# Sparse attention and a soft mixture of experts on one core: where token sums are made, which PSUM banks the plain chunk writes, and which rows of v are kept

## The chip, the cores and the metric

The kernel runs on one core of one Trainium2 chip. The metric is the device time of one execution in microseconds; the figure of the kernel before is the median of three runs. An execution taken by the hardware profiler gives the trace. PE is TensorE (PEld its weight loads), DVE VectorE, ACT ScalarE, POOL GpSimd, SP SyncE; an engine's name with a q at its end means what that engine's queue issues.

## The reference

Batch 4, 8 heads, 768 tokens, head dimension 64, key blocks of 32 tokens (24 blocks). Every query block sees its neighbours, the first and the last block and three sampled blocks; the first and the last query block see everything. The attention output, 3072 tokens of 512 numbers, then goes through four experts of 512 x 1024 x 512, each with a relu, and is summed with the normalised domain probabilities.

```python
mask = np.abs(blk_i - blk_j) <= window
mask = mask | (blk_i == 0) | (blk_j == 0) | (blk_i == n_blocks - 1) | (blk_j == n_blocks - 1)
...
attn = np.exp(scores)
attn = attn / (np.sum(attn, axis=-1, keepdims=True) + 1e-09)
return np.matmul(attn, v).astype(np.float32)
...
for e in range(E):
    h = np.maximum(x @ w1[e], 0.0)
    out += p[:, e:e + 1] * (h @ w2[e])
```

## The kernel before, in words

**Stages.** The attention of batch 0 runs alone. Then a stream of expert work for batch b is interleaved with the attention of batch b + 1, by a fixed cost per piece (`T1` for a piece of the first layer, `T2` for one of the second; `drive`). The experts of batch 3 run alone at the end. From line 673 on every engine keeps the program's order, so what is written earlier stands earlier in each engine's queue.

**The attention** works by units: four edge units (first and last query block) and twelve group units (six groups `t` of up to four query blocks, two halves of the heads). A unit has scores `S` (L251, L256), transposes `T`, the product with v `A` (L291) and the transpose of the output `X`, which ends in the token tile `xr` (L312, L372). A query block's keys come in eight slots of 32 keys: three neighbours, first block, last block, three sampled ones. `copy_k` (L113) copies the five latter into `kr`; `load_v` (L124) fills v tiles for two query blocks at a time: the neighbours by one transfer on SP (L130), the first block's rows by another (L133), and the last block's and the sampled blocks' rows by one indirect gather per query block on GpSimd (L136, 128 rows, indices in `vidx`). The tiles come from a pool that rotates six of them in batch 0 (`v1`, L60) and three later (L733). `load_batch` (L78) takes two tiles of the same pool for the whole v of the batch, which the edge units read. `vidx`, the mask `bad` and the index tile `sbt` are set up ahead of all this (L69 to L218).

**The experts.** Each batch has eight chunks (an expert's 1024 hidden numbers in two). Matmul operands are split into a high part and a rest, and a product is three matmuls (L534 to L539). Chunk 0 is the plain chunk: eight products of two halves each, 16 pieces, on four token operands `xo` 1, 2, 7 and 3. Chunks 1 to 7 save multiplications by sums: 7 products for each of two `s`, on seven token operands, of which 4, 5, 6 and a new 7 are differences of token quarters (`conversion`, L390). `conversion` is a generator of 14 steps. Steps 1 to 6 make the operands 2, 1, 7, 3; steps 7 to 12 make 5, 6 and 4: casts on ScalarE (L399), differences on VectorE or GpSimd (L402), subtractions in place on VectorE (L417, L422, L425, L428). Steps 13 and 14 write operand 7 anew. `convert` (L445) takes the next step, up to a limit.

**The order** is made by `experts` (L619). `one` lists the 114 pieces of the first layer, `two` the 192 of the second (`po` banks, L595, collected into `oacc` by VectorE, L608 and L610). The first 12 pieces of `one` come ahead of any second-layer piece; from there the two mix. When `one` is over, every other second-layer piece takes a step of the next batch's conversion (L638), up to 12. In the first layer every piece below 28 takes a step ahead of its matmuls (L642). For batch 0 three steps are taken in the attention (L722) and two behind it (L743, L744).

**Banks.** After the attention of batch 0, PSUM has two banks for scores, one for attention outputs, and in `ps_m2` one each called v and w, and three called po. The plain chunk writes v and w in turn (L551). When a product is done, `finish` (L541) makes `hh` on ScalarE and `hl` on VectorE out of the bank; only then can the bank take another product. Product i of the plain chunk is pieces 2i and 2i + 1. After products 3, 4, 6 and 7 two weight slabs `wo` are made for later (ScalarE cast L493, GpSimd difference L494); seven slabs are ahead.

```python
ORDER = [(s, n) for s in range(2) for n in (2, 1, 5, 6, 3, 7, 4)]
FIRST = [((0, 0, 0), 0), ((0, 1, 0), 0), ((1, 0, 0), 0), ((0, 0, 1), 2), ((0, 1, 1), 2),
         ((1, 1, 0), 0), ((1, 0, 1), 2), ((1, 1, 1), 2)]
XOF = {(0, 0): 1, (1, 0): 2, (0, 1): 7, (1, 1): 3}
```

Of the kernel before, what the change touches and what calls it, by code (L numbers as in the profile page):

```python
# [8 lines left out]
F32 = mybir.dt.float32  # L9
F32R = mybir.dt.float32r  # L10
I32 = mybir.dt.int32
U32 = mybir.dt.uint32
AF = mybir.ActivationFunctionType
ALU = mybir.AluOpType
# [3 lines left out]
P = 128  # L18
# [5 lines left out]
def attention_moe_kernel(ctx: ExitStack, tc, qb, kb, vr, sampled, sampled_t, probs, w1, w2, out):  # L24
# [42 lines left out]
    sbi = p1.tile([NB, NR, 2], I32, name="sbi")  # L67
    nc.scalar.dma_start(sbi, sampled.bitcast(I32).rearrange("n (r t) -> n r t", t=2))
    sbt = p1.tile([NR + 1, NB, 2], I32, name="sbt")  # L69
    nc.scalar.dma_start(sbt[1:], sampled_t.bitcast(I32).rearrange("r (n t) -> r n t", t=2))  # L70
    sbrow = const.tile([1, NB * NR, 2], I32, name="sbrow")
    nc.scalar.dma_start(sbrow, sampled.bitcast(I32).rearrange("n (r t) -> (n r) t", t=2).unsqueeze(0))

    keys = {}
    gathered = {}
    regs = {}

    def load_batch(b):  # L78
        k = gp.tile([P, NB, P], F32, name="k", bufs=1)
        q = gp.tile([P, 2, P], F32, name="qe", bufs=1)  # L80
        for m in range(2):
            ns = slice(m * NB // 2, (m + 1) * NB // 2)
            nc.sync.dma_start(k[:, ns], kb[b, :, ns])
            if m == 0:
                nc.sync.dma_start(q, qb[b, :, 0:NB:NB - 1])
        vs = []
        for m in range(0, KT, 4):
            n = min(4, KT - m)
            v = pool["v"].tile([P, 2, 2, DM], F32, name="v").rearrange("p a b e -> p (a b) e")
            nc.sync.dma_start(v[:, :n], vr[b * S + P * m:b * S + P * (m + n)]  # L90
                              .rearrange("(k p) e -> p k e", p=P))
            vs += [v[:, i] for i in range(n)]
        keys[b] = k, q, vs
# [13 lines left out]
    def sampled_block(j, r):  # L107
        if (j, r) not in regs:
            regs[j, r] = COPIERS[r % len(COPIERS)].value_load(sbrow[:1, j * NR + r, :1],
                                                              min_val=0, max_val=NB - 1)  # L110
        return regs[j, r]

    def copy_k(b, t, cs=range(QG)):  # L113
        for c, j in enumerate(blocks(t)):
            if c in cs:
                k = pool["k"].tile([P, SLOTS - 3, P], F32, name="kr")
                nc.gpsimd.tensor_copy(k[:, :2], keys[b][0][:, 0:NB:NB - 1])
                for r in range(NR):
                    eng = COPIERS[r % len(COPIERS)]
                    copy = eng.copy if eng is nc.scalar else eng.tensor_copy  # L120
                    copy(k[:, 2 + r:3 + r], keys[b][0][:, bass.ds(sampled_block(j, r), 1)])
                gathered[b, t][1][c] = k

    def load_v(b, t, cs=range(QG)):  # L124
        js = blocks(t)
        for c in range(min(cs), min(max(cs) + 1, len(js)), 2):
            n = min(2, len(js) - c)
            v = pool["v"].tile([P, 2, 2, DM], F32, name="v")
            rows = vr[b * S + (js[c] - 1) * BLOCK:b * S + (js[c] + 2) * BLOCK]
            nc.sync.dma_start(v[:3 * BLOCK, :n, 0],  # L130
                              bass.AP(rows.tensor, rows.offset,
                                      [[DM, 3 * BLOCK], [BLOCK * DM, n], [1, DM]]))
            nc.sync.dma_start(v[3 * BLOCK:, :n, 0],  # L133
                              vr[b * S:b * S + BLOCK].unsqueeze(1).broadcast_to([BLOCK, n, DM]))
            for i in range(n):
                nc.gpsimd.indirect_dma_start(  # L136
                    out=v[:, i, 1], out_offset=None, in_=vr, element_offset=b * S * DM,
                    in_offset=bass.IndirectOffsetOnAxis(ap=vidx[:, js[c + i]:js[c + i] + 1], axis=0))
                gathered[b, t][2][c + i] = v[:, i]


# [16 lines left out]
    nc.gpsimd.affine_select(out=lead, in_=lead, pattern=[[-1, P]], compare_op=ALU.is_ge,  # L158
                            fill=0.0, base=BLOCK - 1, channel_multiplier=BLOCK)
    slot = p1.tile([NR + 1, NB], F32, name="slot")  # L160
    nc.gpsimd.memset(sbt[:1], NB - 1)
    nc.vector.tensor_copy(slot, sbt[:, :, 0])
    within = p1.tile([P, 1], F32, name="within")
    nc.gpsimd.iota(within, pattern=[[0, 1]], base=0, channel_multiplier=1,
# [20 lines left out]
    nc.gpsimd.memset(bad, 0.0)  # L185
    nc.vector.tensor_copy(sbf, sbi[:, :, 0])
    nc.vector.tensor_scalar(bad[:, 3:4], nidx, 1.0, None, op0=ALU.is_le)
    nc.vector.tensor_scalar(bad[:, 4:5], nidx, float(NB - 2), None, op0=ALU.is_ge)
    nc.vector.tensor_scalar(d, sbf, nidx, None, op0=ALU.subtract)
    nc.vector.tensor_mul(d, d, d)  # L190
    nc.vector.tensor_scalar(bad[:, 5:], d, 1.0, None, op0=ALU.is_le)
    nc.vector.scalar_tensor_tensor(d, sbf, float(NB - 1), sbf, op0=ALU.subtract, op1=ALU.mult)
    nc.vector.scalar_tensor_tensor(bad[:, 5:], d, 0.0, bad[:, 5:], op0=ALU.is_equal, op1=ALU.max)
    for r in range(1, NR):
        for e in range(r):
            nc.vector.scalar_tensor_tensor(bad[:, 5 + r:6 + r], sbf[:, r:r + 1], sbf[:, e:e + 1],
                                           bad[:, 5 + r:6 + r], op0=ALU.is_equal, op1=ALU.max)

    ind = p1.tile([NB, NG, P], F32, name="ind")
    nc.gpsimd.memset(ind, 1.0)  # L200
# [237 lines left out]
        xr.pop(b)  # L438
        yield

    EARLY, PLAIN = 3, 12
    pieces = {}
    steps = {}

# [78 lines left out]
    def first(b, c, s, n):  # L523
        ps_m, cp, hp = later["m"], later["c"], later["h"]
        if c == 0:
            half, k, g = n
            w, x = wo[b, c, s, (half, k)], xo[XOF[k, g]]
            if g:
                wo.pop((b, c, s, (half, k)))
        else:  # L530
            w, x = wo.pop((b, c, s, n)), xo[n]

        def product(ps, fresh):
            m = 0  # L534
            for t in range(KH):
                for wi, xi in ((0, 0), (1, 0), (0, 1)):
                    nc.tensor.matmul(ps, w[:, wi, t], x[:, xi, t], start=fresh and m == 0,  # L537
                                     stop=m == 3 * KH - 1, skip_group_check=not fresh)
                    m += 1  # L539

        def finish(half, g, src):  # L541
            hh = hp.tile([P, HS], F32R, name=f"hh{g}", bufs=NH[g])
            hl = hp.tile([P, HS], F32R, name=f"hl{g}", bufs=NH[g])
            nc.scalar.activation(hh, src, AF.Relu)  # L544
            nc.vector.scalar_tensor_tensor(hl, src, 0.0, f32(hh), op0=ALU.max, op1=ALU.subtract)  # L545
            hs[c, 2 * s + half, g] = (hh, hl)

        if c == 0:
            i = [item for item, _ in FIRST].index((s, half, g))
            if k == 0:  # L550
                W[0] = ps_m.tile([P, HS], F32, name="vw"[i % 2], bufs=1)  # L551
            product(W[0], k == 0)
            if k == 1:
                finish(half, g, W.pop(0))
                for _ in range(FIRST[i][1]):
                    next(weights, None)
            return
        if n in (5, 2, 3):
            v = ps_m.tile([P, HS], F32, name="v", bufs=1)
            product(v, True)  # L560
        else:
            if n == 1:
                W[s] = ps_m.tile([P, HS], F32, name="w", bufs=1)
            product(W[s], n == 1)
        if n == 2:
            pt[s] = cp.tile([P, HS], F32, name="p1", bufs=1)
            nc.scalar.copy(pt[s], v)
        elif n == 1:
            nc.vector.tensor_add(pt[s], W[s], pt[s])  # L569
            finish(0, 0, pt[s])  # L570
        elif n == 5:
            zt[s] = cp.tile([P, HS], F32, name="z1", bufs=1)
            nc.scalar.copy(zt[s], v)
        elif n == 6:
            ut[s] = cp.tile([P, HS], F32, name="u1", bufs=1)
            nc.vector.tensor_add(ut[s], W[s], zt[s])
        elif n == 3:
            nc.vector.tensor_add(ut[s], v, ut[s])
            finish(0, 1, ut[s])
        elif n == 7:  # L580
            nc.vector.tensor_add(zt[s], W[s], zt[s])
            finish(1, 1, zt[s])
        else:
            finish(1, 0, W[s])
        next(weights, None)
# [33 lines left out]
    def experts():  # L619

        L = len(ORDER)
        for b in range(B):
# [7 lines left out]
            while q < len(two):  # L630

                wait = after_first and p < len(one) and one[p][2] == 4 and q < ready(p - MORE)
                if wait or p >= min(len(one), (q * NCH * L + (OFF + MORE) * len(two)) / len(two)):
                    second(b, *two[q])
                    q += 1
                    after_first = False
                    if p == len(one) and q % 2:
                        convert(b + 1)  # L638
                    yield T2, 2
                else:  # L640
                    if p < 2 * L:
                        convert(b, PLAIN if p <= L else PLAIN + 2)  # L642
                    first(b, *one[p])
                    p += 1
                    after_first = True
                    yield T1, 1
# [177 lines left out]
```

## Time and profile before

| what | value |
|---|---|
| median of the runs | 1311.59 us (three runs, 1309.81 to 1313.77) |
| profiled execution | 1304.3 us, span 1302.6 us |
| mean granted clock of TensorE | 0.992 |
| busy: TensorE, VectorE, ScalarE, GpSimd | 1252.1, 715.6, 622.6, 659.1 us |
| attention of batch 0 alone | to about 95 us |
| starts of the plain chunk | 96.35, 411.15, about 725 and 1040 us |

The page's second part shows the whole run in 40 slices of 32.6 us. TensorE is short of full in the first four slices and just behind batches' ends.

```profile
PE   7678999999998999999999899999999999999998
...
PEclk9989999999999999999999999999999999999999
DMA  8843334353325124443425231443441322222211
```

A row of the timeline gives the start in us, the duration, the engine, the line, the operation with output and inputs, how many were merged, and in brackets the idle time ahead of it with what ended it. A row of waits gives total, times and longest. A row of windows gives the stretch, its length, busy time and instructions of PE, PEld, DVE, ACT and POOL, the granted clock, the mean busy share of the transfer engines, and GB/s.

### The profile page before, as it was taken

How to read it: one execution, taken by the hardware profiler on the slowest of the kernel's cores; microseconds unless marked ns; L12 is line 12 of the kernel's file. 1: busy time of each engine (PE TensorE's matmuls, PEld its weight loads, DVE VectorE, ACT ScalarE, POOL GpSimd, SP SyncE). 2: the span in 40 equal slices, each digit the busy share in tenths (PEclk: the TensorE clock that was granted, in tenths of full speed). 3: DMA queues.
4: the chain of work that ended last, by engine and by line, in shares of the span. 5: the costliest groups of instructions: out<-in, count | busy, mean ns of one | idle time of the engine just before them, and what ended most of it. 6: DMA issues, size and time to landing. Idle time of an engine off the chain costs nothing.

```text
span 1302.6 us, 31439 instructions
## 1 busy us (share of the span) xinstructions
PE 1252.1 (96%) x12286; PEld 1080.3 (83%) x12286; DVE 715.6 (55%) x1690; ACT 622.6 (48%) x1642; POOL 659.1 (51%) x848
## 2 busy tenths in 40 slices
PE   7678999999998999999999899999999999999998
PEld 4557888888887888888888878888888888888887
DVE  5555655655555555655554555556555545555553
ACT  4673445555543445555554344455554434444441
POOL 5543545566445346654545454566553635454551
PEclk9989999999999999999999999999999999999999
DMA  8843334353325124443425231443441322222211
GB/s 257 240 137 113 91 98 124 113 155 103 98 81 191 49 82 118 136 128 99 145 66 174 97 90 34 139 139 123 123 123 37 105 74 65 65 65 66 65 49 57
DMA packets 60048, 140.49 MB, mean 108 GB/s; under 512 B 7163, under 2 KB 8700, under 8 KB 59900
## 3 DMA queue, kind: packets, MB, share of 16 engines
q1 hardware_dynamic: 52816, 115.41, 28.3%
q0 software_dynamic: 7040, 23.07, 6.4%
q8 instruction: 96, 1.57, 0.5%
q14 instruction: 52, 0.43, 0.1%
q10 hardware_dynamic: 44, 0.00, 0.0%
HBM read 132.17 MB, written 6.29 MB: 106 GB/s over the span
## 4 chain that ended last, share of the span: by engine, by line
PE 90%; DVE 6%; issue 2%; ACT 2%; DVEq 0%; DMA 0%; ACTq 0%
PE po L595 40%; PE w L537 20%; PE v L537 15%; PE o L291 4%; PE tp L278 3%; PE s L256 2%; PE s L251 2%; PE sw L325 1%; DVE oacc L610 1%; DVE xo L402 1%; PE ow L356 1%; PE x L310 1%; DVE hl L545 1%; PE tw L346 1%; DVE xr L422 1%
## 5 line engine op out<-in xcount | busy, mean ns | idle before, releaser
L494 POOL TENSOR_TENSOR wo<-r,wo 128x256 fp32r<-128x256 f32 x368 | 288.8, 788 | 412.0 <-ACT wo L493 411.1
L595 PE MATMUL po<-h,hh 128*128 128x512 f32 x768 | 311.4, 405 | 3.7 <-DVE oacc L610 2.1
L537 PE MATMUL w<-xo,wo 128*128 128x384 f32 x1536 | 310.8, 339 | 1.3 <-DVE hl L545 1.3
L595 PE MATMUL po<-h,hl 128*128 128x512 f32 x768 | 303.9, 396 | 0.0
L595 PE MATMUL po<-l,hh 128*128 128x512 f32 x768 | 303.7, 395 | 0.0
L537 PEld LDWEIGHTS w<-xo,wo 128*128 128x128 f32 x1536 | 275.1, 189 | 22.2 <-DVE hl L545 1.7
L537 PE MATMUL v<-xo,wo 128*128 128x384 f32 x1200 | 244.3, 341 | 13.3 <-DVE hl L545 12.2
L537 PEld LDWEIGHTS v<-xo,wo 128*128 128x128 f32 x1200 | 217.3, 190 | 31.5 <-DVE hl L545 13.8
L493 ACT CAST wo<-r 128x256 fp32r<-128x256 f32 x368 | 146.7, 401 | 157.1 <-DVE r L487 97.7
L510 POOL TENSOR_TENSOR l<-r,h 128x512 fp32r<-128x512 f32 x128 | 171.2, 1338 | 41.9 <-ACT h L509 41.6
L595 PEld LDWEIGHTS po<-h,hl 128*128 128x128 f32 x768 | 144.4, 188 | 33.4
L595 PEld LDWEIGHTS po<-h,hh 128*128 128x128 f32 x768 | 144.3, 188 | 27.2 <-DVE oacc L610 4.7
L595 PEld LDWEIGHTS po<-l,hh 128*128 128x128 f32 x768 | 144.6, 188 | 14.0
L610 DVE SCALAR_TENSOR_TENSOR oacc<-po,pr,oacc 128x512 f32<-128x512 f32 x168 | 121.5, 745 | 15.3 <-PE po L595 14.5
L569 DVE TENSOR_TENSOR p<-w,p 128x384 f32<-128x384 f32 x56 | 31.2, 558 | 161.6 <-PE w L537 161.6
L269 ACT ACTIVATE p<-p,mx 128x256 f32<-128x256 f32 (+1 forms) x192 | 95.4, 498 | 45.5 <-DVE mx L266 45.5
L136 POOL DMA_INDIRECT v<-in_vr_dram,vidx x88 | 86.0, 977 | 45.0 <-issue 16.1
L509 ACT CAST h<-r 128x512 fp32r<-128x512 f32 x128 | 79.4, 621 | 27.2 <-PE po L595 24.8
L494 POOL TENSOR_TENSOR wo<-s,wo 128x256 fp32r<-128x256 f32 x56 | 41.2, 736 | 97.5 <-ACT wo L493 97.5
L266 DVE CUSTOM_DVE_ANT_1 p<-s,mask 128x256 f32<-128x256 f32 (+1 forms) x192 | 69.8, 418 | 35.3 <-PE s L256 35.0
L545 DVE SCALAR_TENSOR_TENSOR hl<-w,hh 128x384 fp32r<-128x384 f32 x72 | 40.1, 557 | 75.4 <-ACT hh L544 75.4
L544 ACT ACTIVATE hh<-p 128x384 fp32r<-128x384 f32 x56 | 29.4, 525 | 91.7 <-DVE p L569 91.7
(115 smaller groups left out, 1406.7 us busy)
## 6 DMA issues: line engine op xcount, KB each, us to landing
r<-in_w_dram SPq DMA_DIRECT2D x64, 512.0 KB, 4.1
r<-in_w_dram SPq DMA_DIRECT2D x128, 256.0 KB, 2.6
v<-in_vr_dram SPq DMA_DIRECT2D x44, 384.0 KB, 4.8
k<-in_kb_dram SPq DMA_DIRECT2D x8, 768.0 KB, 6.7
out_dram<-oacc SPq DMA_DIRECT2D x24, 256.0 KB, 2.7
v<-in_vr_dram SPq DMA_DIRECT2D x44, 128.0 KB, 5.1
q<-in_qb_dram SPq DMA_DIRECT2D x20, 256.0 KB, 5.4
v<-in_vr_dram SPq DMA_DIRECT2D x4, 1024.0 KB, 8.0
```

The costliest lines, as they stand in the source:

```text
L136: nc.gpsimd.indirect_dma_start(out=v[:, i, 1], out_offset=None, in_=vr, element_offset=b * S * DM, in_offset=bass.IndirectOffsetOnAxis(ap= ...
L266: nc.vector.tensor_tensor_reduce(p.rearrange("p (a b) -> p a b", b=BLOCK), s[h][:n, i], mk, -SCALE, 3.0e38, ALU.add, ALU.min, mx[:n])
L269: nc.scalar.activation(p, p, AF.Exp, bias=mx[:n], scale=-1.0, accum_out=self.sums[:n, m:m + 1])
L291: nc.tensor.matmul(o[cs, m], self.pt[:, 2 * m + k, cs], vs[c][:, k, e], start=k == 0, stop=k == 1)
L493: nc.scalar.copy(o[:, 0], src)
L494: nc.gpsimd.tensor_sub(o[:, 1], src, f32(o[:, 0]))
L509: nc.scalar.copy(h, r)
L510: nc.gpsimd.tensor_sub(l, r, f32(h))
L537: nc.tensor.matmul(ps, w[:, wi, t], x[:, xi, t], start=fresh and m == 0, stop=m == 3 * KH - 1, skip_group_check=not fresh)
L545: nc.vector.scalar_tensor_tensor(hl, src, 0.0, f32(hh), op0=ALU.max, op1=ALU.subtract)
L595: nc.tensor.matmul(p, a[:, js], w, start=f == 0 and n == 0, stop=f == FT - 1 and n == 2)
L610: nc.vector.scalar_tensor_tensor(accs[tok], p, pe, accs[tok], op0=ALU.mult, op1=ALU.add)
```

## The change

- `tile_v` gives batch 0 six fixed v tiles, used in turn. The slots of keys and v rows are put in another order (first block, sampled blocks, last block), so that the first and last block's rows share the last 32 partitions of a tile. They are loaded once into each fixed tile when a group first uses it, by two transfers on SP; the gathers of batch 0 bring 96 rows. Later batches gather 128 rows as before, in the new order. The memset of `sbt` stands ahead of its load.
- In batch 0, products 2, 3 and 4 of the plain chunk write `po` banks.
- At the end of a batch only 6 steps of the next conversion are taken (`NEEDED`); in the plain chunk every second piece takes a step, and from piece 16 on every piece.

```diff
-    nc.scalar.dma_start(sbt[1:], sampled_t.bitcast(I32).rearrange("r (n t) -> r n t", t=2))
+    nc.gpsimd.memset(sbt, NB - 1)
+    nc.scalar.dma_start(sbt[:NR], sampled_t.bitcast(I32).rearrange("r (n t) -> r n t", t=2))
...
+    fixed = []
+    turn = [0]
+    filled = set()
+
+    def tile_v(b):
+        if b:
+            return pool["v"].tile([P, 2, 2, DM], F32, name="v"), None
+        i = turn[0] % NFIXED
+        turn[0] += 1
+        if len(fixed) <= i:
+            fixed.append(pool["v"].tile([P, 2, 2, DM], F32, name=f"vf{i}", bufs=1))
+        return fixed[i], i
+
+    NFIXED = 6
...
-            v = pool["v"].tile([P, 2, 2, DM], F32, name="v").rearrange("p a b e -> p (a b) e")
+            v = tile_v(b)[0].rearrange("p a b e -> p (a b) e")
...
-                nc.gpsimd.tensor_copy(k[:, :2], keys[b][0][:, 0:NB:NB - 1])
+                nc.gpsimd.tensor_copy(k[:, 0:NR + 2:NR + 1], keys[b][0][:, 0:NB:NB - 1])
...
-                    copy(k[:, 2 + r:3 + r], keys[b][0][:, bass.ds(sampled_block(j, r), 1)])
+                    copy(k[:, 1 + r:2 + r], keys[b][0][:, bass.ds(sampled_block(j, r), 1)])
...
-            v = pool["v"].tile([P, 2, 2, DM], F32, name="v")
+            v, slot_ = tile_v(b)
...
-            nc.sync.dma_start(v[3 * BLOCK:, :n, 0],
-                              vr[b * S:b * S + BLOCK].unsqueeze(1).broadcast_to([BLOCK, n, DM]))
+            first_ = vr[b * S:b * S + BLOCK].unsqueeze(1)
+            if b:
+                nc.sync.dma_start(v[3 * BLOCK:, :n, 0], first_.broadcast_to([BLOCK, n, DM]))
+            elif slot_ not in filled:
+                filled.add(slot_)
+                nc.sync.dma_start(v[3 * BLOCK:, :, 0], first_.broadcast_to([BLOCK, 2, DM]))
+                nc.sync.dma_start(v[3 * BLOCK:, :, 1], vr[(b + 1) * S - BLOCK:(b + 1) * S].unsqueeze(1)
+                                  .broadcast_to([BLOCK, 2, DM]))
+            hi = P if b else NR * BLOCK
             for i in range(n):
                 nc.gpsimd.indirect_dma_start(
-                    out=v[:, i, 1], out_offset=None, in_=vr, element_offset=b * S * DM,
-                    in_offset=bass.IndirectOffsetOnAxis(ap=vidx[:, js[c + i]:js[c + i] + 1], axis=0))
+                    out=v[:hi, i, 1], out_offset=None, in_=vr, element_offset=b * S * DM,
+                    in_offset=bass.IndirectOffsetOnAxis(ap=vidx[:hi, js[c + i]:js[c + i] + 1], axis=0))
...
-    EARLY, PLAIN = 3, 12
+    EARLY, NEEDED, PLAIN = 3, 6, 12
...
-                W[0] = ps_m.tile([P, HS], F32, name="vw"[i % 2], bufs=1)
+                if b == 0 and 2 <= i < 5:
+
+                    W[0] = ps_m.tile([P, DM], F32, name="po", bufs=HS // P)[:, :HS]
+                else:
+                    W[0] = ps_m.tile([P, HS], F32, name="vw"[i % 2], bufs=1)
...
-                        convert(b + 1)
+                        convert(b + 1, NEEDED)
...
-                    if p < 2 * L:
-                        convert(b, PLAIN if p <= L else PLAIN + 2)
+
+                    if p % 2 or p >= L + MORE:
+                        convert(b, PLAIN if p < L else PLAIN + 2)
```

The columns of `bad` (L187 to L197) move with the slots: 4 to 6 for the sampled blocks, 7 for the last.

## Rows read from the trace of the kernel before

**Rows 1.** The page, part 1: TensorE's busy time and instructions.

```profile
PE 1252.1 (96%) x12286; PEld 1080.3 (83%) x12286; DVE 715.6 (55%) x1690; ACT 622.6 (48%) x1642; POOL 659.1 (51%) x848
```

**Rows 2.** TensorE's waits over the whole run: who waited for whom.

```profile
PE v L537 <- DVE hl L545: 12.2, 5, 3.1
...
PE w L537 <- DVE hl L545: 1.3, 1, 1.3
```

**Rows 3.** The timeline at the start of batch 1's experts.

```profile
409.71 1.93 DVE L422 TENSOR_TENSOR xr<-xr 128x768 f32<-128x768 f32 x1
...
411.15 2.27 PE L537 MATMUL v<-xo,wo 128*128 128x384 f32 x12
...
413.26 2.25 PE L537 MATMUL w<-xo,wo 128*128 128x384 f32 x12
...
414.41 1.38 DVE L402 TENSOR_TENSOR xo<-xr,xo 128x768 fp32r<-128x768 f32 x1
...
415.71 0.94 DVE L428 TENSOR_TENSOR xr<-xr 128x768 f32<-128x768 f32 x1
416.69 0.83 ACT L399 CAST xo<-xr 128x768 fp32r<-128x768 f32 x1 [3.67 <-DVE xr L428]
417.43 0.48 ACT L544 ACTIVATE hh<-v 128x384 fp32r<-128x384 f32 x1
...
417.94 0.56 DVE L545 SCALAR_TENSOR_TENSOR hl<-v,hh 128x384 fp32r<-128x384 f32 x1 [1.29 <-ACT hh L544]
...
418.56 3.17 PE L537 MATMUL v<-xo,wo 128*128 128x384 f32 x12 [3.05 <-DVE hl L545]
...
425.46 1.43 POOL L494 TENSOR_TENSOR wo<-r,wo 128x256 fp32r<-128x256 f32 x2 [6.04 <-ACT wo L493]
...
428.59 0.39 PE L595 MATMUL po<-h,hh 128*128 128x512 f32 x1
```

**Rows 4.** Windows: the two products behind that wait.

```profile
418.56:424.50 5.94, 5.94 (x25) 5.94 (x26) 0.96 (x2) 0.49 (x1) 0.86 (x1) 0.71 0.01 4
```

**Rows 5.** The timeline at the start of batch 0's experts.

```profile
96.35 2.37 PE L537 MATMUL v<-xo,wo 128*128 128x384 f32 x12 [1.12 <-DVE xr L312]
...
97.98 1.89 POOL L402 TENSOR_TENSOR xo<-xr,xo 128x768 fp32r<-128x768 f32 x1 [2.68 <-ACT xo L399]
98.08 2.60 DVE L417 TENSOR_TENSOR xr<-xr 128x768 f32<-128x768 f32 x1
...
102.58 2.36 PE L537 MATMUL v<-xo,wo 128*128 128x384 f32 x12 [1.77 <-DVE hl L545]
...
114.16 0.40 PE L595 MATMUL po<-h,hh 128*128 128x512 f32 x1
```

**Rows 6.** TensorE's waits between 42 and 76 us, in batch 0's attention.

```profile
PE o L291 <- issue: 4.1, 1, 4.1
PE s L251 <- issue: 4.0, 2, 3.1
PE s L256 <- issue: 2.0, 1, 2.0
```

**Rows 7.** Windows: the longest of those waits, and what follows it.

```profile
65.30:69.40 4.10, 0.03 (x3) 0.00 (x0) 0.84 (x6) 1.65 (x8) 3.11 (x6) 0.86 1.06 342
69.40:76.00 6.60, 6.60 (x143) 5.08 (x143) 3.20 (x14) 3.97 (x13) 0.72 (x1) 0.57 0.53 109
```

**Rows 8.** Transfers between 42 and 70 us: total, and v's issues with median us to landing.

```profile
DMA packets 3191, 7.27 MB, mean 260 GB/s; under 512 B 402, under 2 KB 530, under 8 KB 3183
...
v<-in_vr_dram SPq DMA_DIRECT2D x5, 128.0 KB, 7.9
...
v<-in_vr_dram,vidx POOLq DMA_INDIRECT x10, 7.8
```

**Rows 9.** The timeline of SP's queue and of GpSimd: one issue of each kind.

```profile
45.31 0.45 SPq L133 DMA_DIRECT2D v<-in_vr_dram  x1
46.75 0.95 POOL L136 DMA_INDIRECT v<-in_vr_dram,vidx  x1 [0.30 <-DVE kr L121]
```

More of the change, by code (lines that the diff above doesn't have):

```diff
@@ L160, in attention_moe_kernel @@
     slot = p1.tile([NR + 1, NB], F32, name="slot")
-    nc.gpsimd.memset(sbt[:1], NB - 1)
     nc.vector.tensor_copy(slot, sbt[:, :, 0])
@@ L187, in attention_moe_kernel @@
     nc.vector.tensor_scalar(bad[:, 3:4], nidx, 1.0, None, op0=ALU.is_le)
-    nc.vector.tensor_scalar(bad[:, 4:5], nidx, float(NB - 2), None, op0=ALU.is_ge)
+    nc.vector.tensor_scalar(bad[:, 4 + NR:], nidx, float(NB - 2), None, op0=ALU.is_ge)
     nc.vector.tensor_scalar(d, sbf, nidx, None, op0=ALU.subtract)
     nc.vector.tensor_mul(d, d, d)
-    nc.vector.tensor_scalar(bad[:, 5:], d, 1.0, None, op0=ALU.is_le)
+    nc.vector.tensor_scalar(bad[:, 4:4 + NR], d, 1.0, None, op0=ALU.is_le)
     nc.vector.scalar_tensor_tensor(d, sbf, float(NB - 1), sbf, op0=ALU.subtract, op1=ALU.mult)
-    nc.vector.scalar_tensor_tensor(bad[:, 5:], d, 0.0, bad[:, 5:], op0=ALU.is_equal, op1=ALU.max)
+    nc.vector.scalar_tensor_tensor(bad[:, 4:4 + NR], d, 0.0, bad[:, 4:4 + NR], op0=ALU.is_equal, op1=ALU.max)
     for r in range(1, NR):
         for e in range(r):
-            nc.vector.scalar_tensor_tensor(bad[:, 5 + r:6 + r], sbf[:, r:r + 1], sbf[:, e:e + 1],
-                                           bad[:, 5 + r:6 + r], op0=ALU.is_equal, op1=ALU.max)
+            nc.vector.scalar_tensor_tensor(bad[:, 4 + r:5 + r], sbf[:, r:r + 1], sbf[:, e:e + 1],
+                                           bad[:, 4 + r:5 + r], op0=ALU.is_equal, op1=ALU.max)
     ind = p1.tile([NB, NG, P], F32, name="ind")
```

## The prediction

> **What bounds it now.** I read the page first: TensorE is busy 1252.1 of 1302.6 us [rows 1], so only its 50 us of idle, and stretches at half clock, have something to give. Then TensorE's waits over the run [rows 2]: `v` and `w` at L537, the first-layer products, wait 12.2 + 1.3 us for the VectorE pass that makes `hl`, in six waits. The longest, 3.1 us, stands once at the start of each of batches 1 to 3; the other three are batch 0's. Apart from these, TensorE stands still in the attention of batch 0 for reasons called "issue", 10.1 us between 42 and 76 us [rows 6]: the engine waits for no semaphore there.
>
> The timeline of batch 1's start shows what the 3.1 us are [rows 3]. Products 0 and 1 fill banks v and w from 411.15 to 415.4, 2.11 us each. Product 2 wants v back, so `hh` (ScalarE) and `hl` (VectorE) of product 0 must be over. But ahead of that `hh` in ScalarE's in-order queue stands the cast of token sum 4 (L399), which waits for VectorE's subtraction of L428 (415.71), which stands behind the difference of L402 (414.41). So the cast runs at 416.69, `hh` at 417.43, `hl` at 417.94, and product 2 starts at 418.56. After that stop two products, 418.56 to 424.50, run at a mean granted clock of 0.71 [rows 4] and take 5.94 us for 4.2. Batches 2 and 3 repeat it. One start lasts from 411.15 to the second layer at 428.59, 17.44 us; six products at 2.11 are 12.66; it loses **4.8 us**.
>
> In batch 0 [rows 5] one step stands before every product half, and products 2, 3 and 4 each wait, the first 1.77 us. From 96.35 to 114.16 is 17.81 us; less 12.66 it loses 5.15.
>
> **The change, part by part.**
>
> *Token sums step by step.* Nothing is removed: 14 steps before and after, with the same casts (0.83 us) and subtractions (0.94 us undisturbed) [rows 3]. Their place moves. By the code, nine fell into the last 17 second-layer tiles of the batch before, and three ahead of product halves 0, 1, 2; now six fall there and steps 7 to 12 ahead of halves 1, 3, 5, 7, 9, 11. I replay batch 1 with the durations of rows 3. In the tail VectorE has three steps less, so its last sums of `po` are over by 412. The cast of sum 5 has its input ready and runs before 413.3; `hh` of product 0 follows, `hl` ends at 414.4, product 2 may start at 415.4: 1.0 us spare. Step 8 then holds VectorE for 2 x 0.94 us to 416.3, `hl` of product 1 ends at 416.9, wanted at 417.5: 0.6 spare. Step 9 puts a cast that waits for step 8 ahead of `hh` of product 2, from 416.4 to 417.2; product 2 ends at 417.5 only, so the wait holds up nothing behind it. Step 10 is like step 8 (0.6 spare), step 11 like step 9. Step 12 is one GpSimd difference (1.89 us in [rows 5]), first wanted at half 22; GpSimd, which also splits the weights, sat idle 6.04 us before 425.46 [rows 3], and without that cover the step would cost its 1.9 us. With no stop there is no half clock: 3 x 4.8, **14.3 us**.
>
> *Banks.* In batch 0 products 2, 3, 4 go to three `po` banks that nothing holds before the second layer begins, after half 11. Step 6 still takes VectorE 2.60 us beside GpSimd [rows 5], so `hl` of products 0 and 1 end at 101.2 and 102.6, but product 2 no longer asks for them; products 5 and 6 do, at 107 and 109. `hl` of products 2 to 4 end, by the same replay, at 105.0, 106.5 and 109.0; the second layer asks for their banks at 109, 111 and 112. Gain 5.15 less some 0.15 that the first product takes to get going: **5.0 us**; 3 if one of the stops stays.
>
> *v's rows.* Six fixed tiles replace a rotation of six, so a tile is free when it was before. Each of 11 pairs had its own first-block transfer of 128 KB; now six tiles get one of those and one of the last block: 12 issues on SP's queue for 11, 0.45 us each, and GpSimd keeps 22 gathers of 0.95 us [rows 9] with 96 rows for 128. In bytes, groups 0 to 2 move the same 2 MB each, groups 3 and 4 1.5 MB for 2, group 5 0.75 for 1: 1.28 MB less of the 7.27 MB of 42 to 70 us, 18% [rows 8]. Whether that shortens anything rests on the stops of [rows 6]: they come inside a run of matmuls, the transfer engines are full at the longest (share 1.06), and after it the clock is 0.57 for 6.6 us [rows 7], which costs 2.8. I read them as code that comes late behind data. No row shows one under a lighter load. Bounds: all of it goes, 12.9 us gained; one more stop as long as the longest, 4.1 us lost. The load falls by less than a fifth, which lies nearer to the rows as they are: 18% of 12.9, **2.3 us**.
>
> The Trainium skill (Runtime: NRT & Kernel Launch, section Instruction fetch mechanics) says that an engine's instruction fetch runs ahead by itself and that its cost is mostly hidden. The 10.1 us of rows 6 speak against that under full transfer engines. By the page the part would be worth 0, and the sum 19.3 us.
>
> *The rest.* The memset now ahead of the index load, and the swapped columns of `bad`, `kr` and the mask, are as many operations of the same shapes: 0, within half a microsecond either way.
>
> Sum: 14.3 + 5.0 + 2.3 = 21.6 us. The profiled execution took 1304.3 us (1.7 more than its span), so it would take 1282.7. It lies 7.3 us under the median of the runs, 1311.59; I leave that distance as it is: 1311.59 - 21.6, **1290.0 us**. About 0.3%, 3.9 us, can be told from no change.
>
> **Rivals.**
> 1. *Part of the stop stays.* VectorE's subtraction took 1.93 us at 409.71 [rows 3] and 2.60 beside GpSimd [rows 5]. If steps 8 and 10 take 1.93 each time, `hl` of product 1 comes 1.3 us late and that of product 3 another 1.7: 3.0 a batch, 9 in all, 1299. For it: weight splits fall due from half 7 on. Against: GpSimd has nothing to do in halves 0 to 6 of these batches (its idle in [rows 3]). Chance 0.13. The Trainium skill (SBUF — State Buffer, section SBUF: two separate sides) calls the port that the two share an exclusive lock, held for a whole instruction; the 2.60 us beside a GpSimd operation of 1.89 agree with it.
> 2. *The v part gives nothing, or one code stop more.* Batch 0's first three groups move as many bytes as before, and the weights' load comes on top of the fourth; the page's rule above gives the same. 1292.3, up to 1296.4. Against: the fuller the engines, the longer the stops. Chance 0.2.
> 3. *The stops only move on.* If the next chunk's products then wait for sums 5, 6 and 4, what the four starts win is given back: 1308 to 1312. Against: the replay has these ready by half 13, and they are wanted at 18, 19 and 22. Chance 0.05.
> 4. *Slower.* Five VectorE operations of steps 7 to 11 now stand between the `hl` passes. Were GpSimd at work beside each, they would take 2.60 us for 0.94: 8.3 us a batch against 4.8 won, 3.5 lost four times, 1326. It decides where they average above 1.9 us. Against: two splits take GpSimd 1.43 us [rows 3], and four are due there. Chance 0.04.
>
> **The numbers.** The forecast (all four starts free of stops, something from v) has 0.58. Range 1280 to 1300: it goes down to 1280 for most of v's upper bound, and takes in rivals 1 and 2. Faster by over 0.3%: 0.58 + 0.13 + 0.2, less 0.02 for losses not seen, 0.89. Same: rival 3 and a little, 0.06. Slower: rival 4 and a little, 0.05.
>
> **What would show it.** Right: no wait on `hl` at L537; 12.7 us for six products at each of four starts and clock 1.00 after them; casts of sums 5, 6, 4 spread two products apart; fewer "issue" microseconds after 42 us. Wrong: a wait of about 1 us of products 3 or 5 with subtractions of 1.9 us beside GpSimd (rival 1); the same or longer issue stops (rival 2); TensorE waiting for `xo` or `wo` behind the plain chunk (rival 3); subtractions of 2.60 us all along (rival 4).

## The result, and the profile after

The changed kernel takes 1294.1 us in the median of four runs (1293.27 to 1296.25), the kernel before beside it 1312.06 us: a ratio of 0.9871 with a 95% interval of 0.9859 to 0.9884, 18.0 us gained. Forecast were 1290.0 us and 21.6 us of gain, with a range of 1280 to 1300. The sign was right, and the token sums' term with its cause. A second term was given to the wrong part of the change, and the third gave nothing that the runs show.

The page of the changed kernel's profiled execution (1296.25 us) begins so:

```profile
span 1294.5 us, 31441 instructions
## 1 busy us (share of the span) xinstructions
PE 1256.7 (97%) x12286; PEld 1082.2 (84%) x12286; DVE 710.9 (55%) x1690; ACT 625.2 (48%) x1642; POOL 655.4 (51%) x848
```

Against [rows 1] every engine has as many instructions as before. Between these two traces TensorE's idle time falls by 12.7 us and its busy time rises by 4.6. Where idle time went shows in TensorE's waits over the whole run (total, times, longest), which answer to [rows 2]; L537 of before is now L560, L251 and L291 are L274 and L314:

```profile
PE s L274 <- issue: 11.1, 15, 2.6
...
PE o L314 <- issue: 2.9, 3, 1.6
...
```

No first-layer product waits for `hl` any more. The six waits of [rows 2], 13.5 us together, are gone from the list. The issue stops in the attention are not: 14.0 us in these two rows, where the trace of before has 15.7 us in all.

The timeline at the start of batch 1's experts answers to [rows 3] (L422, L425, L440, L445 and L451 are the lines L399, L402, L417, L422 and L428 of before):

```profile
417.46 2.27 PE L560 MATMUL v<-xo,wo 128*128 128x384 f32 x12
...
418.23 0.83 ACT L422 CAST xo<-xr 128x768 fp32r<-128x768 f32 x1
...
419.57 2.24 PE L560 MATMUL w<-xo,wo 128*128 128x384 f32 x12
...
419.77 0.49 ACT L567 ACTIVATE hh<-v 128x384 fp32r<-128x384 f32 x1 [0.70 <-PE v L560]
...
420.30 0.56 DVE L568 SCALAR_TENSOR_TENSOR hl<-v,hh 128x384 fp32r<-128x384 f32 x1 [1.88 <-ACT hh L567]
420.77 0.95 DVE L425 TENSOR_TENSOR xo<-xr,xo 128x768 fp32r<-128x768 f32 x1
...
421.65 2.24 PE L560 MATMUL v<-xo,wo 128*128 128x384 f32 x12
421.75 0.96 DVE L445 TENSOR_TENSOR xr<-xr 128x768 f32<-128x768 f32 x1
...
422.63 0.55 DVE L568 SCALAR_TENSOR_TENSOR hl<-w,hh 128x384 fp32r<-128x384 f32 x1
...
423.73 2.24 PE L560 MATMUL w<-xo,wo 128*128 128x384 f32 x12
...
426.87 1.44 POOL L517 TENSOR_TENSOR wo<-r,wo 128x256 fp32r<-128x256 f32 x2 [7.18 <-ACT wo L516]
...
430.00 0.39 PE L622 MATMUL po<-h,hh 128*128 128x512 f32 x1
```

Products 0, 1, 2 and 3 follow each other 2.1 us apart. The cast of sum 5 is over before `hh` of product 0; `hl` of product 0 is done at 420.9, product 2 comes at 421.65. From the first product to the second layer it takes 12.54 us where [rows 3] had 17.44. The granted clock has no dip behind it, other than in [rows 4]. Windows of the changed kernel over that start:

```profile
417.46:421.70 4.24, 4.24 (x26) 4.23 (x25) 2.36 (x4) 1.85 (x3) 1.51 (x2) 1.00 0.86 250
421.70:430.00 8.30, 8.30 (x50) 8.30 (x49) 6.40 (x10) 4.43 (x9) 2.18 (x3) 1.00 0.36 119
```

TensorE is busy in all of it, at clock 1.00. The starts of batches 2 and 3 take 12.53 us each. In batch 0 the timeline of TensorE answers to [rows 5]:

```profile
106.21 3.90 PE L560 MATMUL v<-xo,wo 128*128 128x384 f32 x12 [1.13 <-DVE xr L335]
109.91 2.30 PE L560 MATMUL w<-xo,wo 128*128 128x384 f32 x12
112.05 6.40 PE L560 MATMUL po<-xo,wo 128*128 128x384 f32 x36
118.28 2.27 PE L560 MATMUL w<-xo,wo 128*128 128x384 f32 x12
120.39 0.39 PE L622 MATMUL po<-h,hh 128*128 128x512 f32 x1
```

There is no wait between the products, and 14.2 us for 17.81. But the experts begin at 106.21 us, not at 96.35 as in the trace of before: nearly ten microseconds later, which the forecast had not seen coming.

### The profile page after: what moved, and what is told of

Same layout as the page of the kernel before. It is cut to its first block, busy times and chain, and to the rows that moved or that the text cites. A ratio compares the mean times of both kernels' runs of the same rounds, so it can differ in the third digit from the quotient of the medians.

```text
span 1294.5 us, 31441 instructions
## 1 busy us (share of the span) xinstructions
PE 1256.7 (97%) x12286; PEld 1082.2 (84%) x12286; DVE 710.9 (55%) x1690; ACT 625.2 (48%) x1642; POOL 655.4 (51%) x848
## 4 chain that ended last, share of the span: by engine, by line
PE 93%; DVE 3%; issue 2%; ACT 1%; POOL 1%; DMA 0%; DVEq 0%; POOLq 0%; ACTq 0%
PE po L622 40%; PE w L560 20%; PE v L560 15%; PE o L314 4%; PE tp L301 3%; PE s L279 2%; PE s L274 2%; PE sw L348 2%; PE ow L379 1%; PE tw L369 1%; DVE oacc L637 1%; PE x L333 1%; ACT p L292 1%; DVE hl L568 1%; PE po L560 0%
## 5 line engine op out<-in xcount | busy, mean ns | idle before, releaser
L560 PE MATMUL w<-xo,wo 128*128 128x384 f32 x1524 | 307.4, 338 | 0.0
L560 PEld LDWEIGHTS w<-xo,wo 128*128 128x128 f32 x1524 | 271.5, 188 | 20.9 <-DVE z L608 0.6
L560 PE MATMUL v<-xo,wo 128*128 128x384 f32 x1176 | 237.1, 338 | 1.1 <-DVE xr L335 1.1
L560 PEld LDWEIGHTS v<-xo,wo 128*128 128x128 f32 x1176 | 211.3, 189 | 17.8 <-DVE xr L335 1.3
L533 POOL TENSOR_TENSOR l<-r,h 128x512 fp32r<-128x512 f32 x128 | 165.2, 1292 | 42.8 <-ACT h L532 42.5
L622 PEld LDWEIGHTS po<-l,hh 128*128 128x128 f32 x768 | 144.4, 188 | 14.2
L160 POOL DMA_INDIRECT v<-in_vr_dram,vidx x66 | 65.3, 990 | 15.4 <-issue 13.5
```

Source lines behind the costliest of these rows:

```text
L160: nc.gpsimd.indirect_dma_start(out=v[:hi, i, 1], out_offset=None, in_=vr, element_offset=b * S * DM, in_offset=bass.IndirectOffsetOnAxis(a ...
L533: nc.gpsimd.tensor_sub(l, r, f32(h))
L622: nc.tensor.matmul(p, a[:, js], w, start=f == 0 and n == 0, stop=f == FT - 1 and n == 2)
```

## The experiments

### One part at a time

The kernel before was traced again, and each part of the change was put into it alone.

> The kernel before, unchanged, for one more trace beside the others. If the attention of batch 0 varies from run to run by as much as the two traces differ (first expert product at 96.35 and at 106.21 us), it starts here anywhere from 96 to 106 us. If the later start comes from the v rows of the change, it starts within 1 us of 96.35. Either way `v` and `w` wait 13.5 us for `hl` at L537.

It took 1313.03 us, and TensorE's timeline at the start of its batch 0 is this:

```profile
105.06 3.81 PE L537 MATMUL v<-xo,wo 128*128 128x384 f32 x12 [1.12 <-DVE xr L312]
...
111.28 2.38 PE L537 MATMUL v<-xo,wo 128*128 128x384 f32 x12 [0.19 <-DVE hl L545]
...
114.98 2.35 PE L537 MATMUL w<-xo,wo 128*128 128x384 f32 x12 [1.32 <-DVE hl L545]
...
118.56 2.36 PE L537 MATMUL v<-xo,wo 128*128 128x384 f32 x12 [1.24 <-DVE hl L545]
...
122.86 0.39 PE L595 MATMUL po<-h,hh 128*128 128x512 f32 x1
```

So the late start comes without the change too. The trace of before on which the prediction rests was of an execution with an uncommonly short attention of batch 0; that is why it took 1304.3 us, below all of the 17 runs of before (1308.16 to 1315.57) made beside this one. From the first expert product on, both traces take the same 1208.0 us to the end. The distance of 7.3 us, left as it was in the forecast, lies there. Of the 8.7 us between the two traces, 5.6 are there at the first score matmul of a group unit (24.26 and 29.82 us); why, the traces were not asked. Two more things differ from [rows 5]: the first product runs at about half clock (3.81 us for 2.1, at a granted clock of 0.57), and product 2 therefore hardly waits.

The steps alone:

```diff
-    EARLY, PLAIN = 3, 12
+    EARLY, NEEDED, PLAIN = 3, 6, 12
...
-                        convert(b + 1)
+                        convert(b + 1, NEEDED)
...
-                    if p < 2 * L:
-                        convert(b, PLAIN if p <= L else PLAIN + 2)
+                    if p % 2 or p >= L + MORE:
+                        convert(b, PLAIN if p < L else PLAIN + 2)
```

> The steps alone: six at the end of a batch, then every second piece; banks and v rows as before. My theory: 14.3 us from batches 1 to 3, and in batch 0 the spread alone removes most of the 4.3 us of waiting, as only product 2 still waits (0.6 us, for the pass of L417); 17 to 19 us faster than before, so ratio 0.986 to 0.987. The rival that part of the stop stays: 9 us less, 0.993. The rival that the stops only move on: within 4 us of before.

Measured: 1294.48 us, ratio 0.9875 (0.9859 to 0.989), 16.4 us by the ratio. This cannot be told from the change's ratio of 0.9871, so the steps alone bring all of its gain that shows. In its list of TensorE's waits there is none for `hl`, in batch 0 neither, with two banks only:

```profile
104.47 4.21 PE L537 MATMUL v<-xo,wo 128*128 128x384 f32 x12 [1.12 <-DVE xr L312]
108.47 3.23 PE L537 MATMUL w<-xo,wo 128*128 128x384 f32 x12
111.54 2.24 PE L537 MATMUL v<-xo,wo 128*128 128x384 f32 x12
113.62 2.24 PE L537 MATMUL w<-xo,wo 128*128 128x384 f32 x12
...
119.88 0.39 PE L595 MATMUL po<-h,hh 128*128 128x512 f32 x1
```

The wait of 0.6 us that I expected of product 2 did not come, because products 0 and 1 took 7.1 us instead of 4.2 here, at a mean granted clock of 0.57 (this kernel's window over them).

The banks alone:

```diff
             if k == 0:
-                W[0] = ps_m.tile([P, HS], F32, name="vw"[i % 2], bufs=1)
+                if b == 0 and 2 <= i < 5:
+                    W[0] = ps_m.tile([P, DM], F32, name="po", bufs=HS // P)[:, :HS]
+                else:
+                    W[0] = ps_m.tile([P, HS], F32, name="vw"[i % 2], bufs=1)
```

> The three borrowed banks alone, steps and v rows as before. Only batch 0 can gain. My theory: products 2 to 4 no longer wait, though the steps still crowd VectorE, and the second layer waits at most 1 us for `hl` of product 3: 3.5 to 5 us faster, ratio 0.996 to 0.9975. If the banks matter only together with the steps: within 1.5 us of before.

Measured: 1310.99 us, ratio 0.9994 (0.9981 to 1.0007): no gain that can be told from none. The timeline of TensorE shows where it went:

```profile
110.77 6.40 PE L537 MATMUL po<-xo,wo 128*128 128x384 f32 x36
...
118.51 0.45 PE L537 MATMUL w<-xo,wo 128*128 128x384 f32 x1 [0.29 <-ACT wo L493]
...
120.04 1.15 PE L537 MATMUL w<-xo,wo 128*128 128x384 f32 x5 [1.09 <-POOL wo L494]
121.02 0.39 PE L598 MATMUL po<-h,hh 128*128 128x512 f32 x1
```

Products 2, 3 and 4 do run through. But ScalarE is as far behind with the steps as before, and the eighth weight slab, which stands in its queue behind the `hh` of product 3, comes late: product 5 waits 1.4 us for it. Beside the waits of 2.75 us in the trace of before above, a little over a microsecond is left, and to the end nothing: from the first product on it takes 1207.9 us here and 1208.0 in the trace of before above.

The v rows alone (the first hunks of the change, with the slots in the new order):

> The v rows alone, with the slot order of the change; steps and banks as before. The forecast's term: 2.3 us faster (ratio 0.998). From the sum that is left over, 18.0 measured less 19.3 for the starts: 1.3 us slower (1.001). If the later start of the experts in the changed kernel's trace is its doing: 8 to 10 us slower (1.007), and the starts would have brought some 27.

Measured: 1313.71 us against 1312.03, ratio 1.0024 (1.001 to 1.0037), 1.3 to 4.9 us slower by the interval. It is not the forecast's 2.3 us of gain, and not the ten microseconds either.

### With and without the v rows

Steps and banks, v rows as before, and beside it the changed kernel once more:

> Steps and banks of the change, v rows as before. The steps alone ran 16.4 us below before and had no wait for `hl` left in any batch, so my theory now is that the banks add nothing beside them: 0.987 to 0.988 of before. The rival, that the v rows cost the 1.3 to 4.9 us that they cost alone and the banks bring them back: 2 to 4 us below the changed kernel run beside it, 0.985.

> The changed kernel once more, on the same chip as the others of this call. If the v rows cost nothing: within 1 us of the steps and banks without them. If they cost what they cost alone: 2 to 4 us above.

Measured: 1293.38 us without the v rows (0.9865, 0.9846 to 0.9884) and 1295.4 us with them (0.9869, 0.9853 to 0.9886). The intervals cover each other. The pair was tried a second time with a change to the load of the first weights, made for another reason:

```diff
-            if n == N - 7:
-                for s in range(2):
-                    load_w1(0, s)
-                for f in range(3):
-                    load_w2(f)
+            if n == N - 8:
+                load_w1(0, 0)
+                load_w2(0)
+            if n == N - 6:
+                load_w1(0, 1)
+                load_w2(1)
+                load_w2(2)
```

> Steps and banks without the v rows, and the first weights (1.75 MB) loaded in two parts at the even units 8 and 10 instead of all at unit 9, beside the fourth group's v. If transfers that come together make the stops long: 1 to 4 us below the version without this. If only the sum of the bytes matters: the same within 1 us.

> Steps, banks and weights in two parts, without the v rows, once more: 1291 to 1293 us, the lowest of the correct versions.

> The changed kernel, v rows among it, with the first weights loaded in two parts at the even units. Against the same without the v rows beside it: if the v rows cost what they cost alone, 1.3 to 4.9 us above; if that was chance, within 1 us; by the forecast's term 2.3 us below.

Without the v rows it took 1291.81 us (0.9852, 0.9838 to 0.9867), and 1294.08 us (0.9863, 0.9846 to 0.988) the second time; with them 1293.6 us (0.9858, 0.9841 to 0.9875) beside the latter. So the first reading, 1.6 us below the version without the spread, did not come again: spreading the weights' load gains nothing that these runs can show, and neither of these versions is shown to beat the change. And beside the steps the v rows make +2.0 us in one pair and -0.5 in the other, neither clear of noise. Alone they cost, by the interval; beside the steps it is open whether they do. A gain of 2.3 us was seen nowhere, and alone the interval excludes it.

The traces show where executions differ. From the first expert product to the end of the execution it takes 1206.4 to 1208.0 us in the four traces with the steps as before, and 1189.4 to 1191.2 in the ten with the steps spread, whatever else they change. So the gain lies behind batch 0's attention, and the rest is when that attention ends: at 103.6 to 107.6 us in the four traces with the v rows and all transfers, at 101.6 to 105.1 in six without the v rows, and at 96.35 in the one that the prediction read.

### What the issue stops are

Why does a fifth less traffic not shorten stops that I had put down to traffic? Three kernels leave transfers out of the changed kernel, all for batch 0's groups 3 to 5, whose tiles keep older rows in their place. The first leaves out both the neighbours' transfers and the gathers:

```diff
+            if b == 0 and t >= 3:
+                for i in range(n):
+                    gathered[b, t][2][c + i] = v[:, i]
+                continue
             nc.sync.dma_start(v[:3 * BLOCK, :n, 0],
```

> The changed kernel, and in batch 0 the v transfers of groups 3 to 5 (neighbours and gathers) left out, so that these groups use rows of earlier groups: 3.8 MB less between 50 and 80 us. If TensorE's issue stops are code that comes late behind data: those after the third group's loads (some 8 us in the changed kernel) fall below 3 us, the experts start 5 to 10 us earlier, time 5 to 10 us lower. If they have another cause: same stops, same time within 2 us. It also bounds from above what the fewer rows of the change could give: they take a third of this away.

Measured: 1283.49 us (0.9786, 0.9771 to 0.9801), 12 us below the changed kernel in the same comparison. So what these transfers do to the attention after the third group is worth about that much; TensorE's mean clock from 50 to 86 us is 0.96 here, and 0.74 in the changed kernel beside it. Two kernels divide it, one without the gathers, one without the neighbours' transfers:

```diff
             for i in range(n):
+                gathered[b, t][2][c + i] = v[:, i]
+                if b == 0 and t >= 3:
+                    continue
                 nc.gpsimd.indirect_dma_start(
```

> The changed kernel with the gathers of batch 0's groups 3 to 5 left out (10 issues, 1.9 MB); the neighbours' transfers stay. In the traces TensorE's issue stops lie in the 5 us in which GpSimd issues the four gathers of a group. If the gathers are what stops it: most of the 12 us that the version without both gained, 1284 to 1287 us. If the bytes are: about half, 1289 to 1290.

```diff
-            nc.sync.dma_start(v[:3 * BLOCK, :n, 0],
-                              bass.AP(rows.tensor, rows.offset,
-                                      [[DM, 3 * BLOCK], [BLOCK * DM, n], [1, DM]]))
+            if b or t < 3:
+                nc.sync.dma_start(v[:3 * BLOCK, :n, 0],
+                                  bass.AP(rows.tensor, rows.offset,
+                                          [[DM, 3 * BLOCK], [BLOCK * DM, n], [1, DM]]))
```

> The changed kernel with the neighbours' transfers of batch 0's groups 3 to 5 left out (5 issues on SP, 1.9 MB); the gathers stay. If the gathers stop TensorE: within 2 us of the changed kernel, 1293 to 1296. If the bytes do: about half of the 12 us, 1289 to 1290.

Without the gathers: 1287.75 us (0.9809, 0.9781 to 0.9836). Without the neighbours' transfers: 1294.65 us (0.9861, 0.9841 to 0.9881), as the changed kernel. The first is somewhat less gain than I had expected of the gathers (1284 to 1287 us). The executions of the two do not overlap (1283.62 to 1289.96, 1292.09 to 1295.03). The same bytes, 1.9 MB, are worth 6.9 us where GpSimd issues them, and nothing that shows where SP does and the gathers stay. Whether the neighbours' transfers cost something once the gathers are gone is not settled: 1287.75 us against the 1283.49 without both, with ratios whose intervals overlap. Windows from 50 to 86 us and TensorE's waits in them, first of the changed kernel run beside the version without both:

```profile
50.00:86.00 36.00, 27.22 (x695) 21.17 (x689) 15.34 (x72) 19.50 (x64) 15.92 (x31) 0.74 0.67 181
...
PE s L274 <- issue: 6.1, 7, 1.2
PE o L314 <- issue: 2.6, 1, 2.6
```

Then of the one without the neighbours' transfers:

```profile
50.00:86.00 36.00, 28.49 (x804) 21.93 (x796) 16.67 (x77) 21.40 (x72) 15.95 (x31) 0.81 0.43 127
...
PE s L275 <- issue: 7.5, 12, 1.2
```

And of the one without the gathers:

```profile
50.00:86.00 36.00, 27.36 (x894) 21.36 (x895) 20.66 (x90) 25.59 (x84) 10.79 (x21) 0.91 0.44 128
...
PE tp L304 <- issue: 3.9, 1, 3.9
...
PE s L282 <- issue: 1.8, 1, 1.8
PE s L277 <- issue: 0.5, 1, 0.5
```

The second and the third have the same load on the transfer engines, 0.43 and 0.44 of their time for 0.67. With the gathers, TensorE stands still twelve times in the score matmuls, for 7.5 us, and its mean clock is 0.81. In the first two windows the stops make up all of TensorE's idle time (8.7 and 7.5 us), so it waits for no result of GpSimd's there, and the work that GpSimd is spared is not on its path. Without the gathers that train of stops is gone. Three stops are left, 6.2 us with 3.9 of it in one, so the sum of the stops fell little in this trace; but TensorE gets through 894 matmuls instead of 804 in the same time, at clock 0.91. The timeline of the version without the neighbours' transfers shows the stops and the gathers side by side:

```profile
50.47 0.94 POOL L161 DMA_INDIRECT vf<-in_vr_dram,vidx  x1 [7.57 <-PE o L315]
...
51.72 0.92 POOL L161 DMA_INDIRECT vf<-in_vr_dram,vidx  x1 [0.30 <-issue]
...
52.95 0.92 POOL L161 DMA_INDIRECT vf<-in_vr_dram,vidx  x1 [0.30 <-ACT pt L304]
...
53.31 0.24 PE L275 MATMUL s<-k,q 64*32 64x96 f32 x1 [0.52 <-issue]
...
54.07 0.24 PE L275 MATMUL s<-k,q 64*32 64x96 f32 x1 [0.52 <-issue]
54.17 0.92 POOL L161 DMA_INDIRECT vf<-in_vr_dram,vidx  x1 [0.30 <-issue]
...
55.52 0.32 PE L275 MATMUL s<-k,q 64*32 64x96 f32 x1 [1.22 <-issue]
...
56.28 0.54 PE L275 MATMUL s<-k,q 64*32 64x96 f32 x6 [0.45 <-issue]
```

While GpSimd issues a group's four gathers, from 50.47 to 55.1, TensorE lets most of its score matmuls go one at a time with 0.2 to 1.2 us between; soon after the last gather they run in rows again. The change keeps the number of gathers and takes rows from each: 0.92 us an issue now, 0.95 in [rows 9]. So at these stops there was little for it to win. What the gather holds up in TensorE, the runs do not show, and gathers alone do not make a train: in the trace that the prediction read, 64 score matmuls from 45.13 us on run without a stop beside two of them.

The single stops are of another kind, and the traces show which. The page lists transfers of code as a kind of their own:

```profile
q8 instruction: 96, 1.57, 0.5%
```

These are 96 packets of 16 KB, and between the starts of two of them TensorE runs 258 matmuls and weight loads in the median, of 24572 in all: the queue is TensorE's. The trace has the time of each packet. Beside the longer single stops:

| trace | TensorE stands still | share of the transfer engines | last code packet landed | TensorE goes on after |
|---|---|---|---|---|
| before, as the prediction read it | 37.13 to 41.03 us | 0.96 | 39.66 | 1.37 us |
| the same | 49.77 to 51.78 | 1.01 | 50.15 | 1.63 |
| the same | 59.94 to 63.08 | 1.04 | 61.76 | 1.32 |
| the same | 65.31 to 69.39 | 1.06 | 67.81 | 1.58 |
| without the gathers | 55.44 to 57.20 | 0.00 | 55.74 | 1.46 |
| the same | 63.92 to 67.82 | 1.01 | 66.46 | 1.36 |
| without the neighbours' transfers | 46.44 to 48.55 | 0.00 | 47.27 | 1.28 |

In the 14 traces, all 38 issue stops of the first 110 us that have no gather in the 3 us before they end, end 1.2 to 1.6 us after a code packet landed, and so do all eight in the trace that the prediction read. In the trains beside gathers that time is anything from 0.1 to 6.3 us, where a packet had landed at all. So the single stops are code that comes late, as far as times alone can show it; no run moved such a packet. Full transfer engines are not needed for one: two of the table come at a share of 0.00, though the longest come at full ones.

## Why the prediction came out as it did

*Token sums, 14.3 us.* Right, by the mechanism given. The starts of batches 1 to 3 take 4.9 us less each (17.44 to 12.54 in the profiled executions), 14.7 us together; against the second trace of before it is 14.2. The replay by durations held: I had `hl` of product 0 end 3.25 us after the start, and it ends 3.4 us after; product 2 wants its bank 4.2 us after the start, both by the replay and in the trace. What the dip of the clock adds to such a stop is not constant: in the second trace of before the three starts take 15.88, 17.28 and 18.67 us, with the same stop of 3.1 us and a granted clock of 1.00, 0.73 and 0.57 in the two products behind it.

*Rival 1.* It did not happen. The subtractions of steps 8 to 10 take 0.95 to 0.96 us, for GpSimd is idle 7.18 us ahead of its next slabs. So what the Trainium skill (SBUF — State Buffer, section SBUF: two separate sides) says of the lock was not put to the test in these starts.

*Banks, 5.0 us.* The failed step is "product 2 no longer asks for them", as the reason why the banks carry the gain of batch 0. Batch 0's start did get shorter, 17.81 to 14.18 us, but with the steps spread no product waits there with two banks either. The banks alone gave 0.8 us, within the noise. Two causes for the gain of batch 0 stood in one sum, and I named only the second. The size came out smaller, 3.6 us between the changed kernel's trace and the second one of before (17.80 to 14.18): in these executions the first product runs at half clock and takes 1.6 us longer, which the one trace did not have, and which hides a part of the waits anyway.

*v's rows, 2.3 us.* They gave nothing that the runs show. The reading "I read them as code that comes late behind data" fits, as to the code, the trace that it was made from: every stop of [rows 6] ends 1.3 to 1.6 us after a code packet landed. The failed step is to take 18% of 12.9 us, as if these stops stood in every execution and shrank with the bytes. In the second trace of before, between 42 and 76 us, one such stop of 1.6 us is left, and 6.4 us are trains beside the gathers, whose number the change leaves alone. In the changed kernel's trace the two kinds take 2.6 and 6.4 us, though the bytes went down about as worked out (7.59 MB between 42 and 90 us for 8.77). So the sign that was named for this term, fewer issue microseconds, did not come. This is rival 2, and its 1292.3 to 1296.4 us hold the 1294.1 measured. Without this term, 14.7 and 3.6 us make 18.3 against 18.0 measured.

The Trainium skill (Runtime: NRT & Kernel Launch, section Instruction fetch mechanics) calls the cost of the fetch mostly hidden. Over the whole run the trace of before agrees: 8 of 96 code packets have a stop behind them. In batch 0's attention these 8 cost 15.7 us, so there the row that I set against the sentence stands. The sum that I drew from it, 19.3 us, lies nearer to the 18.0 measured than mine, but by luck: the stops are there, and the change does not touch them.

*The distance to the median.* Taking it as unchanged held, since it was a matter of the one traced execution: it did not enter the difference of the medians.

## What to carry to other kernels

A cast that waits for another engine's chain, put ahead of the pass that frees a bank in an in-order queue, stops TensorE by the whole chain, and can cost again by a lower clock behind it; spread such steps so that each has a product's time of its own, and replay the queues with the trace's durations to see the spare time. Where two edits remove the same wait, price each alone: the one that removes its cause leaves the other nothing. And before a stop is put down to bytes, take away the same bytes from one issuing engine at a time, see in a second trace whether the stop comes again, and look whether a code packet landed just before it ended.

## What was not expected of the hardware

Leaving out ten gathers issued by GpSimd in the attention gave 6.9 us against the version that leaves out as many bytes issued by SP, and the train of twelve short stops in TensorE's score matmuls went with them. Single stops of up to 4.1 us end 1.2 to 1.6 us after a 16 KB code packet lands, at full and at idle transfer engines. And one kernel's attention of batch 0 ended at 96.35 us in one execution and at 105.06 in another, with the same instructions, so that a single trace's own time can lie 7.3 us below the median of the runs, and its stops can be of another kind than theirs.
